# Thresholds on ScalarE, w1 powers in their own place, and one program order for all engines in batch 2

## The chip, the cores and the metric

The kernel runs on one core of a Trainium2 chip. The metric is the device time of one execution in microseconds (us), the median of several executions. The kernel before takes 1797.5 us (four runs, 1794.0 to 1798.6). A ratio below is the mean time of one kernel's fast runs over that of the other's fast runs of the same rounds, so it is not quite the ratio of the medians that are quoted.

The engines are TensorE (PE in the profile; PEld is its weight load), VectorE (DVE), ScalarE (ACT), GpSimd (POOL) and SyncE (SP), which here only issues DMAs.

## The reference

Threshold attention over 8 batches, 8 heads, 576 rows and head size 64, then a Fourier mixing block with a channel MLP. Cut to what matters:

```python
def _attn_ref(q, k, v, tau):
    scores = np.matmul(q, k.transpose(0, 1, 3, 2)) / np.sqrt(q.shape[-1])
    thresh = np.max(scores, axis=-1, keepdims=True) - tau
    scores = np.where(scores >= thresh, scores, -1e9)
    attn = np.exp(scores - np.max(scores, axis=-1, keepdims=True))
    attn = attn / (np.sum(attn, axis=-1, keepdims=True) + 1e-09)
    return np.matmul(attn, v)

def _moe_ref(x, w_ch1, w_ch2):           # x: (8, 576, 512)
    u = x + np.real(fft(fft(x, axis=1), axis=2))
    un = (u - mean(u)) / np.sqrt(var(u) + 1e-06)
    return u + np.maximum(un @ w_ch1, 0.0) @ w_ch2
```

The two weights come as float64. The chip has to turn them into float32 itself, from their integer halves: mask of the mantissa, copy, low bits, exponent, power of two, sign, two multiplies. That is the "conversion" below. w1 has 16 chunks of 128x512 and w2 has 16.

## The kernel before

A batch is 20 "slots": 4 head pairs of 5 row steps, the fifth of 64 rows. Batch 1 (slots 0 to 19) is written in program order by hand and converts w1. In batch 2 (slots 20 to 39) the channel work of the first rows (matmuls `ph` on `u_t` and w1) runs between the attention slots, and w2 is converted. Here the kernel before holds only TensorE to program order; a scheduler orders the other engines.

```python
    def w2_chunk(j):
        c = 2 * (j % 2)
        raw = u_t[:, c : c + 2, S : S + WC].bitcast(INT32)   # unused columns of u_t
        run = convert(w_ch2[128 * j : 128 * (j + 1), :], w2[j][:, :], raw, nc.gpsimd)
        next(run, None)                                      # issues the load
        return run
    # ... scores(i): transposed scores on TensorE, maxima on VectorE, then
        nc.vector.tensor_scalar(out=thr[:, 0:nh], in0=neg[:, 0:nh], scalar1=-1.0,
                                scalar2=thr_off[:, :], op0=ALU.mult, op1=ALU.add)
        # exp on ScalarE, masked sum on VectorE, +1e-9, reciprocal
    # ... channels(g)
                nc.tensor.matmul(ph[:, 0:GT], w1[c][:, 128 * j : 128 * (j + 1)],
                                 u_t[:, c, c0 : c0 + GT], start=(c == 0), stop=(c == ND - 1))
    # ... batch 2 and later
    chunks = [w2_chunk(j) for j in range(2)]
    by_hand.close()
    ctx.enter_context(tc.manual_schedule(engines={mybir.EngineType.PE}))
    for i in range(per_batch, total + 1):
        if i < total:
            scores(i)
        fill()                                # ph and other channel work
        transposed_weights(i - 1)
        # ...
        if i > per_batch and chunks:
            with tc.issue_after(behind[0].ins):
                for _ in chunks.pop(0):       # a whole chunk
                    pass
            if i - per_batch + 1 < NJ:
                chunks.append(w2_chunk(i - per_batch + 1))
```

A raw chunk lies in two rows of `u_t`, in columns 576 to 1087 of each. `ph` reads columns 0 to 383. No byte is shared, yet a chunk's range from its first to its last byte encloses the columns that `ph` reads in the second row.

## Time and profile before

The stages, cut at the start of the scores of slots 20, 24, 37 and 40 (us, from the profile):

| stage | length | TensorE busy | granted clock |
|---|---|---|---|
| batch 1, slots 0 to 19 | 142.3 | 121.1 | 0.95 |
| slots 20 to 23 (mixing of batch 1) | 48.7 | 34.2 | 0.86 |
| slots 24 to 36 (ph and w2 conversion) | 124.4 | 101.1 | 0.88 |
| slots 37 to 39 | 17.6 | 16.8 | 1.00 |
| from slot 40 | 1463.0 | 1454.8 | 1.00 |

From slot 40 on TensorE is 99% busy. Three of these rows as the profile has them (columns: length; busy us and count of TensorE, weight loads, VectorE, ScalarE, GpSimd; granted clock, DMA share, GB/s):

```profile
0.00:142.34 142.34, 121.09 (x600) 68.44 (x600) 113.80 (x251) 83.53 (x148) 86.75 (x148) 0.95 0.36 100
...
191.06:315.50 124.44, 101.09 (x492) 60.68 (x491) 75.32 (x169) 63.77 (x122) 61.09 (x80) 0.88 0.21 65
...
333.12:1796.00 1462.88, 1454.80 (x6496) 833.53 (x6495) 587.81 (x1465) 446.63 (x936) 192.88 (x408) 1.00 0.08 21
```

### The profile page before, as it was taken

How to read it: one execution, taken by the hardware profiler on the slowest of the kernel's cores; microseconds unless marked ns; L12 is line 12 of the kernel's file. 1: busy time of each engine (PE TensorE's matmuls, PEld its weight loads, DVE VectorE, ACT ScalarE, POOL GpSimd, SP SyncE). 2: the span in 40 equal slices, each digit the busy share in tenths (PEclk: the TensorE clock that was granted, in tenths of full speed). 3: DMA queues.
4: the chain of work that ended last, by engine and by line, in shares of the span. 5: the costliest groups of instructions: out<-in, count | busy, mean ns of one | idle time of the engine just before them, and what ended most of it. 6: DMA issues, size and time to landing. Idle time of an engine off the chain costs nothing.

```text
span 1796.1 us, 21623 instructions
## 1 busy us (share of the span) xinstructions
PE 1728.0 (96%) x7872; PEld 995.9 (55%) x7872; DVE 820.5 (46%) x1985; ACT 626.5 (35%) x1270; POOL 368.1 (20%) x669
## 2 busy tenths in 40 slices
PE   8987787999999999999999999999999999999999
PEld 4545454556556656556556556555556565655453
DVE  7987574634334545544324545543434455521010
ACT  5654464334223334333224333432323333411010
POOL 5664564121110111112101031103011031110000
PEclk9989898999999999999999999999999999999999
DMA  5322122100010110100001110110001010000000
GB/s 153 106 57 68 55 73 67 33 26 20 7 38 14 26 33 14 34 26 20 13 26 27 26 27 20 27 32 14 14 26 27 19 27 20 1 12 6 12 6 18
DMA packets 130352, 57.03 MB, mean 32 GB/s; under 512 B 121123, under 2 KB 121125, under 8 KB 130246
## 3 DMA queue, kind: packets, MB, share of 16 engines
q1 hardware_dynamic: 126550, 46.96, 10.0%
q0 software_dynamic: 2304, 8.39, 1.4%
q8 instruction: 63, 1.03, 0.2%
q10 hardware_dynamic: 1392, 0.30, 0.1%
q14 instruction: 43, 0.35, 0.1%
HBM read 46.02 MB, written 9.44 MB: 31 GB/s over the span
## 4 chain that ended last, share of the span: by engine, by line
PE 86%; DVE 8%; ACT 3%; issue 1%; DMA 1%; SPq 1%; POOL 1%; ACTq 0%; DVEq 0%; POOLq 0%
PE ph L685 27%; PE po L706 27%; PE pv L503 9%; PE sc L394 7%; PE pw L482 6%; PE sc L405 2%; DVE e L429 2%; DVE neg L416 1%; PE py L594 1%; PE pa L611 1%; PE pe L468 1%; PE pn L669 1%; ACT e L426 1%; PE pa L615 1%; PE pe L469 1%
## 5 line engine op out<-in xcount | busy, mean ns | idle before, releaser
L685 PE MATMUL ph<-u_t,w 128*128 128x384 f32 x1536 | 531.8, 496 | 27.9 <-ACT u_t L303 27.1
L706 PE MATMUL po<-w,h 128*128 128x512 f32 x1152 | 524.2, 597 | 0.0
L685 PEld LDWEIGHTS ph<-u_t,w 128*128 128x128 f32 x1536 | 285.1, 192 | 220.0 <-ACT u_t L303 26.9
L426 ACT ACTIVATE e<-sc,neg 128x576 f32<-128x576 f32 x288 | 204.2, 738 | 487.0 <-DVE neg L416 485.6
L416 DVE TENSOR_REDUCE neg<-sc 128x1 f32<-128x576 f32 x288 | 205.8, 751 | 317.3 <-PE sc L394 226.8
L706 PEld LDWEIGHTS po<-w,h 128*128 128x128 f32 x1152 | 208.0, 190 | 222.0 <-issue 220.9
L429 DVE SCALAR_TENSOR_TENSOR e<-sc,thr,e 128x576 f32<-128x576 f32 x288 | 225.9, 815 | 39.2 <-ACT e L426 26.0
L438 POOL COPY rec<-den 128x128 f32<-128x128 f32 x160 | 50.2, 314 | 769.5 <-DVE den L436 443.1
L394 PE MATMUL sc<-kT,qT 64*128 64x288 f32 x1024 | 169.6, 442 | 5.3 <-DVE e L429 4.0
L482 PE MATMUL pw<-ident,e 128*128 128x128 f32 x1152 | 157.0, 276 | 10.8 <-DVE x L508 3.4
L691 ACT ACTIVATE h<-ph 128x384 f32<-128x384 f32 x96 | 47.0, 490 | 290.6 <-PE ph L685 290.6
L484 ACT COPY e_t<-pw 128x512 f32<-128x512 f32 x256 | 139.0, 592 | 7.4 <-PE pw L482 3.6
L394 PEld LDWEIGHTS sc<-kT,qT 64*128 64x128 f32 x1024 | 93.6, 192 | 85.4 <-issue 61.1
L482 PEld LDWEIGHTS pw<-ident,e 128*128 128x128 f32 x1152 | 132.7, 142 | 14.5 <-ACT tmp L626 4.1
L693 DVE TENSOR_SCALAR h<-ph 128x384 f32<-128x384 f32 x96 | 53.3, 555 | 184.1 <-PE ph L685 183.8
L508 DVE TENSOR_TENSOR x<-pv,ends 128x288 f32<-128x288 f32 x64 | 29.0, 455 | 172.4 <-PE pv L503 172.4
L472 ACT COPY ends<-pe 128x256 f32<-128x256 f32 x128 | 47.7, 373 | 138.0 <-PE pe L469 129.4
L713 DVE SCALAR_TENSOR_TENSOR u<-po,rstd,u 128x512 f32<-128x512 f32 x36 | 26.9, 748 | 132.4 <-PE po L706 132.4
L503 PE MATMUL pv<-e_t,v_in 128*64 128x288 f32 x512 | 68.3, 409 | 0.0
L503 PE MATMUL pv<-e_t,v_rev 128*64 128x288 f32 x512 | 68.3, 409 | 0.0
L420 DVE TENSOR_SCALAR thr<-neg,thr_off 128x2 f32<-128x2 f32 (+1 forms) x160 | 52.0, 325 | 5.2
L442 POOL COPY e<-e 128x64 f32<-128x64 f32 x32 | 7.8, 242 | 226.6 <-DVE e L429 163.3
(143 smaller groups left out, 1543.5 us busy)
## 6 DMA issues: line engine op xcount, KB each, us to landing
out_dram<-u SPq DMA_DIRECT2D x36, 256.0 KB, 2.0
qk_in<-in_q_dram SPq DMA_DIRECT2D x64, 128.0 KB, 2.4
stage<-in_moe_w_ch_dram SPq DMA_DIRECT2D x16, 512.0 KB, 4.2
v_in<-in_v_dram SPq DMA_DIRECT2D x64, 128.0 KB, 2.3
u_t<-in_moe_w_ch_dram POOLq DMA_DIRECT2D x16, 512.0 KB, 3.9
qk_in<-in_k_dram SPq DMA_DIRECT2D x31, 128.0 KB, 2.4
qk_in<-in_k_dram SPq DMA_DIRECT2D x31, 64.0 KB, 2.3
qk_in<-in_k_dram SPq DMA_DIRECT2D x93, 16.0 KB, 2.0
```

What stands on the lines that cost most here:

```text
L394: nc.tensor.matmul(sc[j][:, c, 0:HALF], qT[hp, 128 * t : 128 * t + 128], kT[hp, HALF * c : HALF * (c + 1)], start=True, stop=True,)
L416: nc.vector.tensor_reduce(out=neg[:, j : j + 1], in_=sc[j][:, :, 0:HALF], axis=AXIS_XY, op=ALU.max, negate=True,)
L420: nc.vector.tensor_scalar(out=thr[:, 0:nh], in0=neg[:, 0:nh], scalar1=-1.0, scalar2=thr_off[:, :], op0=ALU.mult, op1=ALU.add,)
L426: nc.scalar.activation(out=ej, in_=sc[j][:, :, 0:HALF], func=ACT.Exp, bias=neg[:, j : j + 1], scale=1.0)
L429: nc.vector.scalar_tensor_tensor(out=ej, in0=sc[j][:, :, 0:HALF], scalar=thr[:, j : j + 1], in1=ej, op0=ALU.is_ge, op1=ALU.mult, accum_out ...
L438: nc.gpsimd.tensor_copy(rec[:, :].rearrange("p (j d) -> p j d", j=nh), _repeated(den[:, 0:nh], 2 * D // nh))
L482: nc.tensor.transpose(pw[:, c, :], e[:, c0 : c0 + 128], ident[:, :])
L484: nc.scalar.copy(e_t[:, 4 * j : 4 * j + 4, qs], pw[:, :, :])
L503: nc.tensor.matmul(pv[64 * j : 64 * j + 64, 0:HALF], vt[:, 2 * c + j, :], e_t[:, 4 * j + c, cols] if c < 4 else ends[:, 0, cols], start=(c ...
L685: nc.tensor.matmul(ph[:, 0:GT], w1[c][:, 128 * j : 128 * (j + 1)], u_t[:, c, c0 : c0 + GT], start=(c == 0), stop=(c == ND - 1),)
L693: nc.vector.tensor_relu(ht, ph[:, 0:GT])
L706: nc.tensor.matmul(po[:, :], hT[j // 4][:, j % 4, 128 * t : 128 * (t + 1)], w2[j][:, :], start=(j == 0), stop=(j == NJ - 1),)
```

## The change

It means to free VectorE in batch 1 (threshold on ScalarE, exponents taken early, folding and centring spread over several steps) and to keep the hand-made order of all engines through batch 2. The w2 loads move from GpSimd's queue to SyncE's. The cuts leave out three smaller parts: in batch 1 the weighted values of a head pair now stand between the two halves of a slot's softmax, a slot that is filled up with dummy matmuls has one instead of two from slot 16 on, and the mixing of batch 1 is begun a step earlier. The core of the diff, with cuts:

```diff
-        nc.vector.tensor_scalar(
-            out=thr[:, 0:nh], in0=neg[:, 0:nh], scalar1=-1.0, scalar2=thr_off[:, :],
-            op0=ALU.mult, op1=ALU.add,
-        )
         for j in range(nh):
             # exp of half j on ScalarE
+            if j == 0:
+                nc.scalar.activation(
+                    out=thr[:, 0:nh], in_=neg[:, 0:nh], func=ACT.Identity,
+                    bias=thr_off[:, :], scale=-1.0,
+                )
             # masked sum of half j on VectorE, and now +1e-9 for each half
@@ convert (w1 gets its own place for the powers; w2 stays in place)
-        queue.dma_start(out=raw, ...)
+        nc.sync.dma_start(out=raw, ...)
         # mask of the mantissa
+        if not in_place:
+            exponents()
@@ the 64-row slot
-            nc.gpsimd.tensor_copy(e[:, S : S + 64], e[:, 512:S])
+            nc.scalar.copy(e[:, S : S + 64], e[:, 512:S])
@@ batch 2
-    by_hand.close()
-    ctx.enter_context(tc.manual_schedule(engines={mybir.EngineType.PE}))
     for i in range(per_batch, total + 1):
+        if i == 2 * per_batch:
+            by_hand.close()
+            ctx.enter_context(tc.manual_schedule(engines={mybir.EngineType.PE}))
         if i < total:
             scores(i)
+        under_way = [chunks[m] for m in (i - per_batch, i - per_batch - 1) if m in chunks]
+        for run in under_way:          # mask of chunk j; low bits, exponents of chunk j - 1
+            next(run, None)
         fill()
         transposed_weights(i - 1)
+        for run in under_way:          # copy of chunk j; power and sign of chunk j - 1
+            next(run, None)
         # ...
+        j = i - per_batch - 1
+        if j in chunks:
+            next(chunks.pop(j), None)  # the two multiplies of chunk j on GpSimd
+            if j + 2 < NJ:
+                chunks[j + 2] = w2_chunk(j + 2)
```

More of the change, by code (lines that the diff above doesn't have):

```diff
@@ L268, with convert @@
     nc.vector.memset(shift[:], -float((1023 - 127) << 23))
-    def convert(src, dst, raw, queue):
+    def convert(src, dst, raw, power):
         if src.dtype == FP32:
-            queue.dma_start(out=dst, in_=src)
+            nc.sync.dma_start(out=dst, in_=src)
             return
-        queue.dma_start(out=raw, in_=src.bitcast(INT32).rearrange("p (c n) -> p c n", c=2))
+        nc.sync.dma_start(out=raw, in_=src.bitcast(INT32).rearrange("p (c n) -> p c n", c=2))
         pairs = raw.rearrange("p c (n two) -> p c n two", two=2)
@@ L280, in convert, with add_low, exponents, powers_and_signs @@
         bits = dst.bitcast(INT32)
+        in_place = power is None
+        power = low if in_place else power.rearrange("p (c n) -> p c n", c=2)
+        sign = high.bitcast(FP32)
+        def add_low():
+            nc.vector.scalar_tensor_tensor(
+                out=dst, in0=low.bitcast(UINT32), scalar=2.0**-52, in1=dst,
+                op0=ALU.mult, op1=ALU.add,
+            )
+        def exponents():
+            nc.vector.tensor_scalar(
+                out=power, in0=high, scalar1=20, scalar2=0x7FF,
+                op0=ALU.logical_shift_right, op1=ALU.bitwise_and,
+            )
+        def powers_and_signs():
+            nc.scalar.activation(
+                out=power, in_=power, func=ACT.Relu, bias=shift[:, :], scale=float(1 << 23)
+            )
+            nc.scalar.activation(out=sign, in_=high, func=ACT.Sign)
         yield
@@ L285, in convert @@
         )
+        if not in_place:
+            exponents()
         yield
         nc.scalar.activation(out=dst, in_=bits, func=ACT.Copy, bias=1.0, scale=2.0**-20)
+        if not in_place:
+            powers_and_signs()
         yield
-        nc.vector.scalar_tensor_tensor(
-            out=dst, in0=low.bitcast(UINT32), scalar=2.0**-52, in1=dst, op0=ALU.mult, op1=ALU.add
-        )
-        nc.vector.tensor_scalar(
-            out=low, in0=high, scalar1=20, scalar2=0x7FF,
-            op0=ALU.logical_shift_right, op1=ALU.bitwise_and,
-        )
-        yield
-        nc.scalar.activation(
-            out=low, in_=low, func=ACT.Relu, bias=shift[:, :], scale=float(1 << 23)
-        )
-        sign = high.bitcast(FP32)
-        nc.scalar.activation(out=sign, in_=high, func=ACT.Sign)
+        add_low()
+        if in_place:
+            exponents()
+        yield
+        if in_place:
+            powers_and_signs()
         yield
-        nc.gpsimd.tensor_tensor(out=dst, in0=dst, in1=low.bitcast(FP32), op=ALU.mult)
+        nc.gpsimd.tensor_tensor(out=dst, in0=dst, in1=power.bitcast(FP32), op=ALU.mult)
         nc.gpsimd.tensor_tensor(out=dst, in0=dst, in1=sign, op=ALU.mult)
@@ L310, in w1_chunk @@
         cols = slice(WC * g, WC * (g + 1))
-        stage = sb.tile([128, 2, WC], INT32, tag=f"h{n % 4}", bufs=1, name="stage")
-        run = convert(w_ch1[128 * c : 128 * (c + 1), cols], w1[c][:, cols], stage, nc.sync)
+        stage = sb.tile([128, 3, WC], INT32, tag=f"h{n % 4}", bufs=1, name="stage")
+        run = convert(
+            w_ch1[128 * c : 128 * (c + 1), cols], w1[c][:, cols], stage[:, 0:2, :], stage[:, 2, :]
+        )
         next(run, None)
@@ L319, in w2_chunk @@
         raw = u_t[:, c : c + 2, S : S + WC].bitcast(INT32)
-        run = convert(w_ch2[128 * j : 128 * (j + 1), :], w2[j][:, :], raw, nc.gpsimd)
+        run = convert(w_ch2[128 * j : 128 * (j + 1), :], w2[j][:, :], raw, None)
         next(run, None)
@@ L326 @@
     means = {}
+    prs = {}
     def column_means(g):
@@ L338, in mirrored @@
         cols = slice(WC * g, WC * (g + 1))
-        means[g] = means[g], []
+        prs[g] = []
         for c in (1, 3):
@@ L342, in mirrored @@
             nc.tensor.matmul(pr[:, :], mirror[:, :], w1[c][:, cols], start=True, stop=True)
-            means[g][1].append(pr)
+            prs[g].append(pr)
     def less_mean(eng, g, c):
         cols = slice(WC * g, WC * (g + 1))
-        mean, prs = means[g]
-        rows = prs[c // 2][:, :] if c % 2 else w1[c][:, cols]
-        eng.tensor_tensor(out=w1[c][:, cols], in0=rows, in1=mean[:, :], op=ALU.subtract)
+        rows = prs[g][c // 2][:, :] if c % 2 else w1[c][:, cols]
+        eng.tensor_tensor(out=w1[c][:, cols], in0=rows, in1=means[g][:, :], op=ALU.subtract)
     heads = {}
     steps = {}
-    behind = [None]
     xs = {}
@@ L382, in prep_pair, with scores @@
             load_pair(n + 1)
-    def scores(i):
+    def scores(i, between=None):
         n, t = divmod(i, NT)
@@ L419, in scores @@
             )
-        nc.vector.tensor_scalar(
-            out=thr[:, 0:nh], in0=neg[:, 0:nh], scalar1=-1.0, scalar2=thr_off[:, :],
-            op0=ALU.mult, op1=ALU.add,
-        )
         for j in range(nh):
@@ L428, in scores @@
             )
+            if j == 0:
+                nc.scalar.activation(
+                    out=thr[:, 0:nh], in_=neg[:, 0:nh], func=ACT.Identity,
+                    bias=thr_off[:, :], scale=-1.0,
+                )
             nc.vector.scalar_tensor_tensor(
@@ L432, in scores @@
             )
-        nc.vector.tensor_scalar(
-            out=den[:, 0:nh], in0=den[:, 0:nh], scalar1=1e-9, scalar2=None, op0=ALU.add
-        )
-        behind[0] = nc.vector.reciprocal(den[:, 0:nh], den[:, 0:nh])
+            nc.vector.tensor_scalar(
+                out=den[:, j : j + 1], in0=den[:, j : j + 1], scalar1=1e-9, scalar2=None,
+                op0=ALU.add,
+            )
+            if between is not None:
+                between()
+                between = None
+        nc.vector.reciprocal(den[:, 0:nh], den[:, 0:nh])
         rec = sb.tile([128, 2 * D], FP32, tag="rec", name="rec")
@@ L531, in fold_rows @@
             eng.tensor_tensor(out=half[:, c, 1:HALF], in0=up, in1=down, op=op)
+        yield
         for c, c0, op in (
@@ L547, in fold_rows @@
         )
+        yield
         if n % NPAIR == 1:
@@ L755, in step @@
         n, t = divmod(i, NT)
-        scores(i)
         if t == 1 and n > 0:
-            weighted_values(n - 1)
+            scores(i, lambda: weighted_values(n - 1))
             load_v(n + 1)
+        else:
+            scores(i)
+        if t == 1 and n > 0:
+            pass
         elif later and later[0][0] <= i:
-            later.pop(0)[1]()
+            later.pop(0)[1](i)
         else:
-            busy(2)
+            busy(2 if i < NCHUNK else 1)
         if t == NT - 1:
@@ L773, in step @@
                 next(chunks[k], None)
-        while after:
-            after.pop(0)()
+        while after and after[0][0] <= i:
+            after.pop(0)[1]()
         if i - 1 in chunks:
@@ L779, in step @@
             chunks[i + 3] = w1_chunk(i + 3)
-        if t == 3 and n > 0:
-            fold_rows(n - 1)
+        if t == 2 and n > 0:
+            folds.append(fold_rows(n - 1))
+        if folds and next(folds[0], True):
+            folds.pop(0)
+    folds = []
     later = []
@@ L787, in center, with first, second @@
     def center(g):
-        def first():
+        def first(i):
             column_means(g)
-            after.append(lambda: copy_mean(g))
-        def second():
+            after.append((i, lambda: copy_mean(g)))
+        def second(i):
             mirrored(g)
-            for c in range(ND):
-                after.append(lambda c=c: less_mean(nc.vector if c % 2 else nc.gpsimd, g, c))
+            for c, eng, wait in (
+                (1, nc.vector, 0), (3, nc.vector, 0), (0, nc.gpsimd, 1), (2, nc.gpsimd, 2)
+            ):
+                after.append((i + wait, lambda c=c, eng=eng: less_mean(eng, g, c)))
         later.append((ND * g + 6, first))
@@ L820 @@
     while later:
-        later.pop(0)[1]()
+        later.pop(0)[1](per_batch)
     while after:
-        after.pop(0)()
-    chunks = [w2_chunk(j) for j in range(2)]
-    by_hand.close()
-    ctx.enter_context(tc.manual_schedule(engines={mybir.EngineType.PE}))
+        after.pop(0)[1]()
+    while folds:
+        if next(folds[0], True):
+            folds.pop(0)
+    chunks = {j: w2_chunk(j) for j in range(2)}
     for i in range(per_batch, total + 1):
+        if i == 2 * per_batch:
+            by_hand.close()
+            ctx.enter_context(tc.manual_schedule(engines={mybir.EngineType.PE}))
         if i < total:
             scores(i)
+        under_way = [chunks[m] for m in (i - per_batch, i - per_batch - 1) if m in chunks]
+        for run in under_way:
+            next(run, None)
         fill()
@@ L837 @@
         fill()
-        if i > per_batch and chunks:
-            with tc.issue_after(behind[0].ins):
-                for _ in chunks.pop(0):
-                    pass
-            j = i - per_batch + 1
-            if j < NJ:
-                chunks.append(w2_chunk(j))
+        j = i - per_batch - 1
[3 more added lines that the diff above has]
+                chunks[j + 2] = w2_chunk(j + 2)
         fill()
@@ L847 @@
             weighted_values(n - 1)
-            fold_rows(n - 1)
+            for _ in fold_rows(n - 1):
+                pass
             if n + 1 < B * NPAIR:
@@ L853 @@
             mixes.append(mixing(b))
+            if b == 0:
+                next(mixes[0])
             todo += MIX
```

## The prediction

> **What bounds the kernel now.** I read the page's slices first, then busy time in hand-chosen stretches, then the waits of TensorE, then the instructions in order of time.
>
> ```profile
> PE   8987787999999999999999999999999999999999
> PEclk9989898999999999999999999999999999999999
> ```
>
> TensorE has room only in the first seven slices of 44.9 us. Cut by stage (columns: busy us of TensorE, weight loads, VectorE, ScalarE, GpSimd, then granted clock, DMA share, GB/s):
>
> ```profile
> 45.00:142.00 97.00, 84.48 (x446) 48.44 (x446) 81.95 (x175) 59.30 (x106) 62.40 (x79) 0.93 0.27 75
> 142.00:191.00 49.00, 34.51 (x206) 23.35 (x205) 31.11 (x73) 22.21 (x45) 24.10 (x29) 0.86 0.27 74
> 191.00:316.00 125.00, 101.65 (x495) 61.13 (x496) 75.79 (x171) 63.77 (x122) 61.24 (x81) 0.88 0.21 65
> ...
> 331.00:1796.00 1465.00, 1456.92 (x6504) 834.41 (x6502) 588.80 (x1467) 448.34 (x940) 192.88 (x408) 1.00 0.08 21
> ```
>
> A "slot" is one 128-row step of attention, 20 to a batch. Batch 1 (slots 0 to 19) ends near 142 us: VectorE is busy 84% and does scores and w1 conversion in one queue. Slots 24 to 36 of batch 2 lie between 191 and 316 us: TensorE idles 23.4 us and runs at clock 0.88. After 331 us it is 99% busy. So the end is "end of batch 2 plus a fixed 1465 us", and only the first 331 us can change.
>
> What TensorE waits for from 155 to 331 us (total, times, longest):
>
> ```profile
> PE ph L685 <- ACT u_t L303: 27.1, 9, 5.5
> PE py L594 <- DVE den L433: 4.9, 1, 4.9
> ```
>
> L303 is the last ScalarE step of converting a w2 chunk, which lies raw in unused columns of u_t. The channel matmuls (ph) read other columns of u_t, yet wait for it. One such wait in order of time (start, us):
>
> ```profile
> 272.77 2.29 PE L394 MATMUL sc<-kT,qT 64*128 64x288 f32 x8
> 275.09 1.42 DVE L416 TENSOR_REDUCE neg<-sc 128x1 f32<-128x576 f32 x2 [4.55 <-PE sc L394]
> ...
> 280.05 0.16 DVE L436 RECIPROCAL den<-den 128x2 f32<-128x2 f32 x1
> 280.12 0.41 DVE L283 TENSOR_SCALAR w<-u_t 128x512 int32<-128x512 int32 x1
> ...
> 281.23 0.69 DVE L289 SCALAR_TENSOR_TENSOR w<-u_t,w 128x512 f32<-128x512 uint32 x1 [0.70 <-ACT w L287]
> 282.02 0.43 DVE L294 TENSOR_SCALAR u_t<-u_t 128x512 int32<-128x512 int32 x1
> 282.48 0.74 ACT L299 ACTIVATE u_t<-u_t,shift 128x512 int32<-128x512 int32 x1 [1.29 <-DVE u_t L294]
> 283.13 0.65 ACT L303 ACTIVATE u_t<-u_t 128x512 f32<-128x512 int32 x1
> ...
> 283.83 4.21 PE L685 MATMUL ph<-u_t,w 128*128 128x384 f32 x6 [3.62 <-ACT u_t L303]
> ```
>
> Scores, softmax on VectorE, conversion, then ph, one after the other in one slot; and ph then takes 4.21 us for what took 2.10 at 265.97 us. The wait also costs clock.
>
> In batch 1 the threshold op shows a second cost:
>
> ```profile
> L294 DVE TENSOR_SCALAR stage<-stage 128x512 int32<-128x512 int32 x15 | 9.7, 645 | 0.5
> L420 DVE TENSOR_SCALAR thr<-neg,thr_off 128x2 f32<-128x2 f32 x14 | 9.5, 682 | 0.5
> ...
> L420 DVE TENSOR_SCALAR thr<-neg,thr_off 128x1 f32<-128x1 f32 x4 | 0.9, 214 | 0.1
> ```
>
> Two elements take 682 ns on average, one takes 214: beside 1.29 us GpSimd multiplies the two-element op stands waiting.
>
> **What the Trainium skill says.** "SBUF — State Buffer", Who interferes with whom: two-port VectorE ops such as tensor_scalar and GpSimd take a shared port pair in turn, each for a whole instruction. The 682 against 214 ns agrees. "TensorE: Matmul & The Clock Gate", Part 1: after an idle window of about 3.4 us the array falls to half clock until it has been busy as long. Agrees: 3.62 us idle, then 4.21 for 2.10. "ScalarE: Activation LUTs", What ACT_TABLE_LOAD costs: an ACTIVATE with a pointer bias takes about 280 ns plus 0.83 ns an element. No such two-element op is in this trace; I take 0.28 us as an estimate.
>
> **The change, part by part.** I read dependencies from the order and semaphore targets of the built programs, durations from the trace.
>
> *Batch 1.* thr leaves VectorE: 14 x 0.68 us. In its place VectorE waits for ScalarE's exp and then thr: the maxima end 1.42 us after the scores, thr at about 1.75, so about 0.38 us of idling. Gain 14 x 0.3 = 4 us. The +1e-9 becomes two one-element ops (about 0.16 each) for one of 0.24: loss 14 x 0.1 = 1.4. GpSimd starts its multiplies earlier, so mask and exponent ops (586 and 645 ns on average, 0.41 and 0.43 undisturbed) lose perhaps half of their waits: gain 15 x 0.2 = 3. Weighted values now stand between the two halves of a slot: x waits for 5 us of pv matmuls before the second half's mask and all conversion; loss about 0.8 in each of 3 slots, 2.4. Folds and centring in pieces and fewer dummy matmuls are beside VectorE's chain: 0. Sum: 3 us gained.
>
> *Slots 20 to 23.* From VectorE's first sum (170.87) to the ph that can run (187.1) it takes 16.2 us through GpSimd. After: ten adds of 0.75, two multiplies of 1.29, one copy of 0.33, two more adds: about 12. No DMA issue (0.75 each) is left on GpSimd. Gain about 4.
>
> *Slots 24 to 36*, where the result is decided. In the new program order a slot is: scores(i), mask of chunk j, then low bits and exponents of chunk j-1 on VectorE; ScalarE's power and sign of chunk j-1 follow in the same slot. The false dependency stays: all 14 ph groups in slots 24 to 36 wait for a conversion step of their own slot (9 for the sign, and 5, in slots 28 to 32, for the exponent op), and scores(i+1) stand behind ph. Before, the scheduler put most conversions ahead of the next slot's scores; only four groups (slots 24, 32, 33, 34) waited within their slot, and slots like 26, 27 and 36 took about 5.5 us.
>
> The new chain from the end of sc: maxima to reciprocal 1.42 + 0.38 + 2 x 0.82 + small ops 0.65 = 4.1; mask 0.41, low bits 0.70, exponents 0.43: 5.65; power and sign 0.74 + 0.65: 7.1. (The conversion alone: 3.0 instead of 3.65, as the ScalarE round trip inside is gone.) At full clock a slot with one ph matmul left is sc 1.24 + 7.1 + 0.9 = 9.3; with three left, 10.5; a slot that waits for the exponents needs 1.24 + 5.7 + 0.9 to 2.1 + transposes 1.2 = 9.1 to 10.2; a 64-row slot about 1.8 less; pv adds 5.0 to three slots. Summed over the 13 slots, with 1.4 for one preparation, 2.6 for two table loads, and ScalarE late by 1 to 3 us in slots 30 and 32: about 147 us, against 124.4 now (191.13 to 315.50). That is 22 us lost at full clock. Three-matmul slots idle 4 to 5 us, so half clock may add up to 3 us in each of five: up to 15 more.
>
> *After 331 us*: thr and the 64-column copy on ScalarE (35% busy), w2 loads gone from GpSimd's queue: 0.
>
> Sum: -3 - 4 + 22 to 37 = +15 to +30. The walk has no slack in it where a step is out of order, but it contradicts what the author of such a change must hope for, so I lean towards the low end and below it: 1797.6 + 14, about 1812.
>
> **Rivals.** (1) The new order removes the 27.1 us of ph waits: conversion steps are spread and shorter, and all engines follow one order. For it: these waits are the largest idle item. Against: the semaphore targets show the waits still there, and more of them within the slot. It would make 1765 to 1785. (2) Nothing moves: TensorE work is fixed, both orders hide as much; batch 1 gains what batch 2 loses: 1790 to 1802. (3) The full half-clock loss: ph and scores at half speed through all of batch 2: 1830 to 1840.
>
> **Range and chances.** 1812, 8 in 10 between 1780 and 1834. 2% is 36 us: faster by that needs all of rival 1 and more (0.05); slower needs rival 3 (0.12); the rest 0.83.
>
> **What would show it.** In the new profile TensorE's wait of ph for ScalarE's sign op and for VectorE's exponent op should total 35 us or more over 11 or more waits; the stretch of slots 24 to 36 should be 140 us or longer with a granted clock below 0.88; batch 1 should end 0 to 6 us earlier; the stretch after batch 2 should stay 1465 us within 5. I am wrong if that stretch of batch 2 is shorter than 124 us, which would mean the conversion runs ahead of the scores after all, or if batch 1 alone gains over 10 us.

## The result

The changed kernel takes 1845.5 us (median of four runs, 1844.6 to 1848.6), against 1797.5 us. The ratio is 1.0273, with a 95% interval from 1.0255 to 1.0292: slower, and above the range of the prediction.

The page's slices of the profile after. The third to seventh slices are the ones to look at:

```profile
PE   8986656799999999999999999999999999999999
...
PEclk9997778899999999999999999999999999999999
```

One slice is 46.1 us now. TensorE's busy share falls to 5 and 6 tenths and its clock to 7 tenths where the kernel before had 7 to 8 and 8 to 9; everything behind is as before.

The same stretches of the changed kernel, same columns:

```profile
0.00:135.12 135.12, 116.90 (x605) 67.70 (x605) 102.27 (x250) 87.10 (x174) 85.66 (x143) 1.00 0.38 104
...
184.76:360.98 176.22, 116.56 (x491) 66.02 (x490) 70.39 (x169) 67.46 (x140) 52.92 (x68) 0.80 0.17 50
...
377.02:1842.80 1465.78, 1455.04 (x6496) 833.28 (x6495) 557.09 (x1438) 474.94 (x1084) 186.63 (x383) 1.00 0.08 21
```

Batch 1 ends 7.2 us earlier. Slots 24 to 36 hold the same matmuls (491, and 492 before) but take 51.8 us longer: 36.3 us more of idle TensorE (59.7 against 23.4) and 15.5 us more of busy time at the lower clock. From slot 40 on it is 2.8 us longer.

TensorE's longest waits in the first 400 us of the changed kernel (total us, times, longest):

```profile
PE ph L714 <- ACT u_t L304: 31.1, 10, 6.0
PE ph L714 <- DVE u_t L293: 29.2, 5, 9.0
```

L304 is the sign op and L293 the exponent op of a w2 chunk. The kernel before had 27.1 us in 9 waits, all for the sign op. These are 60.3 us in 15 waits. The new order made the wait that it should have removed more frequent.

The longest of them in order of time (start, us, engine; SPq is SyncE's DMA queue):

```profile
249.77 1.28 POOL L326 TENSOR_TENSOR w<-w,u_t 128x512 f32<-128x512 f32 x1
...
251.47 0.16 DVE L463 RECIPROCAL den<-den 128x1 f32<-128x1 f32 x1
...
253.56 0.56 SPq L277 DMA_DIRECT2D u_t<-in_moe_w_ch_dram  x1
257.21 0.43 DVE L308 TENSOR_SCALAR w<-u_t 128x512 int32<-128x512 int32 x1 [5.58 <-DMA u_t<-in_moe_w_ch_dram]
257.55 0.68 DVE L287 SCALAR_TENSOR_TENSOR w<-u_t,w 128x512 f32<-128x512 uint32 x1
258.34 0.43 DVE L293 TENSOR_SCALAR u_t<-u_t 128x512 int32<-128x512 int32 x1
...
258.82 4.21 PE L714 MATMUL ph<-u_t,w 128*128 128x384 f32 x6 [8.97 <-DVE u_t L293]
```

The softmax of the slot is done at 251.6. The mask op (L308) of the next chunk then waits 5.58 us for its raw data, which came only 3.65 us after their load was issued. The last multiply (L326) had freed the buffer at 251.05, and the load was issued at 253.56: q and k loads stood ahead of it on SyncE's queue for these 2.5 us. That part is an exception; the other w2 loads of this stretch were issued at most 0.6 us after their buffer came free. In VectorE's program order the low bits (L287) and the exponents (L293) of the chunk before stand behind that mask, and `ph` stands behind them. In slots 24 to 36 the mask waits for a load four times:

```profile
DVE w L308 <- DMA u_t<-in_moe_w_ch_dram: 10.7, 4, 5.6
```

The kernel before has no such wait in this stretch. This is a second loss beside the one foreseen.

### The profile page after: what moved, and what is told of

Its sections match the earlier page's. It is cut to its first block, busy times and chain, and to the rows that moved or that the text cites. A ratio compares the mean times of both kernels' runs of the same rounds, so it can differ in the third digit from the quotient of the medians.

```text
span 1842.8 us, 21678 instructions
## 1 busy us (share of the span) xinstructions
PE 1739.3 (94%) x7870; PEld 1000.5 (54%) x7870; DVE 768.6 (42%) x1953; ACT 659.6 (36%) x1462; POOL 346.9 (19%) x621
## 4 chain that ended last, share of the span: by engine, by line
PE 80%; DVE 5%; ACT 3%; DMA 1%; POOL 1%; issue 1%; SPq 0%; DVEq 0%; ACTq 0%
PE ph L714 27%; PE po L735 26%; PE pv L530 8%; PE sc L415 6%; PE pw L509 5%; PE sc L426 2%; DMA u_t<-in_moe_w_ch_dram 1%; DVE e L451 1%; PE py L623 1%; DVE neg L437 1%; PE pa L640 1%; ACT e L443 1%; PE pn L698 1%; PE pa L644 1%; PE pe L495 1%; PE pe L496 1%
## 5 line engine op out<-in xcount | busy, mean ns | idle before, releaser
L714 PE MATMUL ph<-u_t,w 128*128 128x384 f32 x1536 | 544.5, 504 | 61.6 <-ACT u_t L304 31.1
L443 ACT ACTIVATE e<-sc,neg 128x576 f32<-128x576 f32 x288 | 211.4, 734 | 540.9 <-DVE neg L437 539.7
L499 ACT COPY ends<-pe 128x256 f32<-128x256 f32 x128 | 47.5, 371 | 95.5 <-PE pe L496 89.0
L558 POOL TENSOR_TENSOR half<-x 128x287 f32<-128x287 f32 x48 | 38.1, 816 | 89.6 <-DVE x L535 62.2
L530 PEld LDWEIGHTS pv<-e_t,v_rev 128*64 128x64 f32 x512 | 36.3, 141 | 33.5 <-issue 10.2
```

The lines of the kernel that those rows point to most:

```text
L443: nc.scalar.activation(out=ej, in_=sc[j][:, :, 0:HALF], func=ACT.Exp, bias=neg[:, j : j + 1], scale=1.0)
L499: nc.scalar.copy(ends[:, :, qs], pe[:, 0:2, :])
L530: nc.tensor.matmul(pv[64 * j : 64 * j + 64, 0:HALF], vt[:, 2 * c + j, :], e_t[:, 4 * j + c, cols] if c < 4 else ends[:, 0, cols], start=(c ...
```

## The experiments

Fourteen kernels ran, each with runs of the kernel before on the same chip. "a_" names start from the changed kernel, "b_" names from the kernel before. All times by stage come from one profile each. Kernels with the changed batch 1 left as it is ended it between 134.4 and 137.8 us, so a single figure of batch 1 is good to about 2 us; the other stages repeat within about 1 us in the few pairs with the same code there (slots 20 to 23 of the changed kernel and a_busy, slots 24 to 36 of the kernel before and b_power).

| kernel | batch 1 | slots 20-23 | 24-36 | 37-39 | from 40 | median us |
|---|---|---|---|---|---|---|
| before | 142.3 | 48.7 | 124.4 | 17.6 | 1463.0 | 1797.5 |
| changed | 135.1 | 49.6 | 176.2 | 16.0 | 1465.8 | 1845.5 |
| a_sched2 | 135.3 | 47.6 | 128.2 | 17.3 | 1466.2 | 1796.8 |
| a_pool_dma | 137.7 | 49.2 | 171.6 | 17.4 | 1465.9 | 1844.5 |
| a_own_raw | 137.8 | 46.2 | 134.0 | 17.3 | 1465.8 | 1799.4 |
| b_own_raw | 143.9 | 47.5 | 106.1 | 17.5 | 1463.1 | 1782.7 |
| a_own3 | 136.6 | 46.3 | 119.1 | 16.0 | 1465.8 | 1785.7 |
| a_thr_dve | 136.7 | 50.1 | 176.2 | 17.4 | 1462.9 | 1845.0 |
| b_thr_act | 137.5 | 47.7 | 128.5 | 17.4 | 1466.1 | 1801.2 |
| b_power | 139.7 | 49.1 | 124.6 | 17.7 | 1463.0 | 1794.5 |
| best | 135.9 | 47.5 | 101.9 | 17.4 | 1463.0 | 1766.7 |
| a_first | 137.0 | 50.3 | 124.2 | 18.5 | 1465.8 | 1795.2 |
| a_busy | 135.8 | 50.6 | 171.1 | 16.0 | 1465.8 | 1841.6 |
| a_own3_thr | 136.3 | 46.3 | 120.4 | 17.2 | 1463.0 | 1783.3 |
| a_noload | 135.6 | 46.8 | 160.2 | 17.5 | 1465.7 | 1831.4 |
| a_noload_busy | 134.4 | 47.7 | 156.5 | 16.0 | 1465.7 | 1823.8 |

**Is it the order of batch 2? (a_sched2)** Batch 2 as in the kernel before, everything else as changed.

```diff
+    chunks = [w2_chunk(j) for j in range(2)]
+    by_hand.close()
+    ctx.enter_context(tc.manual_schedule(engines={mybir.EngineType.PE}))
     for i in range(per_batch, total + 1):
-        if i == 2 * per_batch: ...            # and the under_way steps
+        # a whole chunk behind the reciprocal; loads on nc.gpsimd
```

> The changed kernel with batch 2 as in the kernel before: program order held on TensorE alone from slot 20 on, each w2 chunk converted whole behind the reciprocal, w2 loads on GpSimd's queue. Theory (the loss of 51.8 us in slots 24 to 36 comes from the fixed order of batch 2, and batch 1 keeps its gain of 7.2 us): slots 24 to 36 back to 120 to 130 us, batch 1 still ending near 135 us, 1786 to 1798 us in all. Rival (the loss comes from thresholds on ScalarE or the other single changes, which remain here): slots 24 to 36 stay above 150 us, 1825 us or more.

Measured: 1796.8 us, ratio 1.0000 (0.9985 to 1.0015). Slots 24 to 36 are back to 128.2 us. The loss is in the order of batch 2, with the loads' queue. But the batch 1 gain of 7 us does not show in the total: 3.8 us more in slots 24 to 36 and 3.3 us more after slot 40 eat it. What does that comes below (b_thr_act).

**Is it the loads' queue? (a_pool_dma)** Having seen ten q and k loads ahead of the w2 load on SyncE's queue, I moved it.

```diff
-        nc.sync.dma_start(out=raw, ...)
+        queue = nc.gpsimd if power is None else nc.sync
+        queue.dma_start(out=raw, ...)
```

> The changed kernel with only the w2 loads moved back to GpSimd's queue. Theory (a w2 load on SyncE's queue stands behind ten q and k loads that wait for the pair's transposes, so the raw chunk lands late): VectorE's 10.7 us of waits of the mask op for that load in slots 24 to 36 vanish, and with them some half-clock time: 1825 to 1838 us. Rival (the raw buffer comes free late anyway, so that the queue doesn't matter, and an issue of 0.74 us on GpSimd delays the multiplies): 1843 to 1850 us.

Measured: 1844.5 us. My theory falls and the rival holds: VectorE's waits for loads did not vanish (15.1 us in 7 waits from 130 to 365 us, and 16.7 in 7 in the changed kernel). Its slots 24 to 36 are 4.6 us shorter, but its batch 1 and slots 37 to 39, where nothing was changed, are 4.0 us longer, so a gain is not shown. The Trainium skill, "Trainium Kernel Development and Optimization", Key Constraints, says that DMAs issued from several engines share the same DMA engines and that issuing from more of them saves only issue time. That agrees: a w2 load took 3.8 us from issue to landing on GpSimd's queue and 3.7 on SyncE's, and the times are 1844.5 and 1845.5 us.

**Is it the false dependency? (a_own_raw, b_own_raw)** There is no room for two more buffers of 4 KB per partition. But the last rows of w2 are empty until the last chunks are converted, so raw chunks 0 to 11 can lie there. Chunks 12 to 15 stay in `u_t`. (A first version for 13 chunks gave NaN values.)

```diff
-    w2 = [const.tile([128, DM], FP32, name=f"w2_{j}") for j in range(NJ)]
+    w2_all = const.tile([128, NJ, DM], FP32, name="w2_all")
+    w2 = [w2_all[:, j, :] for j in range(NJ)]
@@ w2_chunk
+        if j < NJ - 4:
+            r = NJ - 4 + 2 * (j % 2)
+            raw = w2_all[:, r : r + 2, :].bitcast(INT32)
```

> The changed kernel with the raw w2 chunks 0 to 11 in the rows of w2 that are filled last, not in unused columns of u_t (chunks 12 to 15 stay in u_t). Theory (the ph matmuls wait for conversions only because both lie in one box of u_t): the waits of ph in slots 24 to 32, 44.8 us in all, fall below 8 us; those of slots 33 to 36, 12.5 us, stay; clock of the stretch rises from 0.80 above 0.9; 1795 to 1815 us. Rival (the fixed order of the engines is what binds: without this wait TensorE waits as long for the softmax of the next slot): less than 15 us gained, 1830 us or more.

> The kernel before with the same move of the raw w2 chunks 0 to 11 out of u_t. Theory (the same false dependency costs the kernel before 14.2 us of waits in slots 25 to 32 and half-clock time behind them): 1775 to 1786 us. Rival (the scheduler's order fills the gap with other work, or the wait is taken over by the softmax): 1790 to 1799 us.

Measured: a_own_raw 1799.4 us, ratio 1.0009 to the kernel before, that is 46 us less than the changed kernel; b_own_raw 1782.7 us, ratio 0.9919 (0.9900 to 0.9937). Both theories hold, but for the clock of the stretch, which came to 0.88 in a_own_raw and not above 0.9. The waits of TensorE in slots 24 to 36 of a_own_raw:

```profile
PE pe L500 <- POOL rec L469: 13.9, 2, 8.0
PE ph L718 <- ACT u_t L305: 13.7, 4, 5.4
```

Only the four chunks left in `u_t` still hold `ph` back. In place of the others a new wait stands first, of the transposes for the broadcast reciprocal. A cause that fits is in VectorE's waits (a_own3 below tests it):

```profile
DVE w_all L309 <- DMA w_all<-in_moe_w_ch_dram: 19.5, 8, 4.7
```

Without the false dependency the slots are shorter, the loads are later relative to them, and VectorE holds the next softmax behind a mask that waits for its data. The same stretch of b_own_raw, columns as in the stage lines above:

```profile
191.30:297.37 106.07, 92.15 (x492) 56.25 (x491) 76.53 (x171) 63.61 (x122) 58.02 (x77) 0.93 0.23 67
```

**Are two raw buffers too few? (a_own3)** One row more for `w2_all`, which the 2 KB left allow, makes three buffers.

```diff
-    w2_all = const.tile([128, NJ, DM], FP32, name="w2_all")
+    w2_all = const.tile([128, NJ + 1, DM], FP32, name="w2_all")
-            r = NJ - 4 + 2 * (j % 2)
+            r = NJ - 5 + 2 * (j % 3)
-    chunks = {j: w2_chunk(j) for j in range(2)}
+    chunks = {j: w2_chunk(j) for j in range(3)}    # and loads issued three chunks ahead
```

> As a_own_raw, with three raw buffers for chunks 0 to 11 in place of two, each load issued three chunks ahead. Theory (a chunk's conversion now spans two slots, so two buffers leave a load only the time from the last multiply to the next slot's mask op, and VectorE stands waiting for the load in order, with the next reciprocal behind it): VectorE's waits of the mask op for loads, 24.9 us in a_own_raw, fall below 6, those of the transposes for the broadcast reciprocal (13.9 us) below 2, slots 24 to 36 from 134 to 112 to 122 us; 1778 to 1790 us. Rival (the waits pass to the softmax of the next scores): no more than 5 us gained, 1794 us or more.

Measured: 1785.7 us, 13.7 us less. Over the first 400 us VectorE's waits for w2 loads fell from 24.9 to 3.2 us, and slots 24 to 36 take 119.1 us. The wait for the reciprocal fell only to 6.5 us, not below 2, so late loads were a part of it and not all:

```profile
DVE w_all L309 <- DMA w_all<-in_moe_w_ch_dram: 3.2, 1, 3.2
...
PE pe L500 <- POOL rec L469: 6.5, 2, 3.7
```

The Trainium skill, "Trainium Kernel Development and Optimization", Best Practices, says to double-buffer. Here a conversion reaches over two slots, and two buffers leave no slot for the load; this run shows that the third is worth 13.7 us.

**What is the threshold worth? (a_thr_dve, b_thr_act)** The threshold op put back, and the threshold op moved alone.

```diff
 # a_thr_dve: threshold on nc.vector ahead of the exponentials, as before
 # b_thr_act: on nc.scalar behind the first exponential, as changed
```

> The changed kernel with the threshold op back on VectorE ahead of the exponentials; everything else stays. Theory (the threshold op gave batch 1 about 4 us): batch 1 ends 3 to 6 us later, at 138 to 142 us; in batch 2 the chain of a slot gets about 0.2 us shorter; 1843 to 1849 us. Rival (thresholds on ScalarE bring nothing in batch 1, and the gain comes from the order of the rest): batch 1 ends at 134 to 137 us and the total falls below 1843 us.

> The kernel before with thresholds on ScalarE behind the first exponential, and nothing else. Theory: batch 1 ends 3 to 5 us earlier than at 142.3; about 2 us are lost after slot 40, where ScalarE gets later; 1792 to 1797 us. Rival (VectorE waits for ScalarE's exponential and threshold as long as its own op took): batch 1 ends at 141 to 144 us, 1798 to 1802 us.

Measured: b_thr_act 1801.2 us, ratio 1.0023 (1.0011 to 1.0035). Batch 1 ends 4.9 us earlier, as expected, but slots 24 to 36 take 4.0 us longer and the part from slot 40 3.1 us longer, so the move alone loses. a_thr_dve 1845.0 us: taking it out of the changed kernel leaves batch 1 at 136.7, which is inside the spread of 134.4 to 137.8, against the theory, and gives the 2.9 us after slot 40 back. So both readings held in part: alone the move gives 4.9 us, beside the rest hardly anything. The group lines of VectorE in the first 135 us fit this, first the kernel before, then the changed kernel (busy us, mean ns, then idle time before and its cause):

```profile
L420 DVE TENSOR_SCALAR thr<-neg,thr_off 128x2 f32<-128x2 f32 x16 | 11.3, 708 | 0.6
...
L451 DVE SCALAR_TENSOR_TENSOR e<-sc,thr,e 128x576 f32<-128x576 f32 x36 | 29.3, 813 | 13.4 <-ACT thr L447 12.9 <-POOL half L558 0.4
...
L308 DVE TENSOR_SCALAR w<-stage 128x512 int32<-128x512 int32 x16 | 7.6, 476 | 1.1 <-DMA stage<-in_moe_w_ch_dram 1.1
```

then a_thr_dve:

```profile
L441 DVE TENSOR_SCALAR thr<-neg,thr_off 128x2 f32<-128x2 f32 x16 | 7.4, 463 | 0.6
```

With the rest of the change in place the threshold op costs VectorE 463 ns and not 708 ns as in the same stretch before, 7.4 us in all. What takes its place is 12.9 us of waiting for ScalarE, where a_thr_dve has 3.6.

**What are the powers worth? (b_power)** Only the w1 powers in their own place.

```diff
-        stage = sb.tile([128, 2, WC], INT32, tag=f"h{n % 4}", bufs=1, name="stage")
+        stage = sb.tile([128, 3, WC], INT32, tag=f"h{n % 4}", bufs=1, name="stage")
 # and convert() of the changed kernel; w2 in place and on nc.gpsimd as before
```

> The kernel before with only the w1 powers in a place of their own, so that VectorE takes the exponents with the mask, a step earlier, and ScalarE does power and sign with the copy. Theory of the prediction (earlier multiplies on GpSimd give about half the waits of mask and exponent ops): batch 1 ends 2 to 3 us earlier, 139 to 140.5 us; 1794 to 1797 us. Rival (this step alone is worth as much as the whole gain of batch 1, as the chain of a chunk loses a round trip): batch 1 ends at 135 to 138 us, 1790 to 1794 us.

Measured: 1794.5 us, ratio 0.9980 (0.9966 to 0.9995), batch 1 at 139.7. Of the parts that were run alone it is the only one that gains in the total. Its 2.7 us in batch 1 are hardly more than the 2 us to which such a figure is good, and the upper end of its interval is close to 1.

**Fixed order, or place in the slot? (a_first)** All engines stay in program order and the raw data stay in `u_t`; the whole conversion of a chunk stands ahead of the slot's scores.

```diff
+        j = i - per_batch - 1
+        if j in chunks:
+            for _ in chunks.pop(j):
+                pass
+            if j + 2 < NJ:
+                chunks[j + 2] = w2_chunk(j + 2)
         if i < total:
             scores(i)
-        under_way = ...                       # and the steps behind
```

> The changed kernel with program order on all engines in batch 2 kept, raw chunks still in u_t, but each chunk converted whole, in one slot, ahead of that slot's scores and softmax. Theory (what costs is the place of the conversion behind the softmax of its own slot, not the fixed order as such): the waits of ph for conversion steps in slots 24 to 36 fall from 57.3 to under 25 us, VectorE's waits for loads vanish since the load gets a slot more, slots 24 to 36 take 125 to 145 us, 1795 to 1815 us. Rival (a fixed order with chunks in u_t costs as much in either place, as the softmax is now late): 1830 us or more.

Measured: 1795.2 us, ratio 0.9985 (0.9970 to 1.0000), slots 24 to 36 in 124.2 us. It came out slightly below the low end of the slots' range. The waits of `ph` for conversion fell from 57.3 to 18.1 us, and VectorE waited for no load:

```profile
PE ph L714 <- ACT u_t L304: 18.1, 9, 4.2
```

A fixed order is not what costs; conversion behind the softmax of its own slot, spread over two slots, is. The run changes the place, the spread and the loads' time at once, so it does not say how much each of them costs; nor was this order tried with the raw data out of `u_t`.

**What does the half clock cost? (a_busy)** Five dummy matmuls a slot keep TensorE busy in its waits.

```diff
             scores(i)
+            if per_batch + 3 < i < 2 * per_batch - 3:
+                busy(5)
```

> The changed kernel with five dummy matmuls behind the scores in slots 24 to 36, so that TensorE does not idle long enough to fall to half clock; all waits stay. Theory (15.5 us of the loss are matmuls at half clock, 116.6 us of busy time for the same 491 matmuls that took 101.1): the granted clock of the stretch rises from 0.80 above 0.9 and the time falls by 5 to 15 us, to 1830 to 1841 us. Rival (the clock does not set the end, as the ends of the slots hang on VectorE's chain alone, or the dummies delay as much as they save): 1843 us or more.

Measured: 1841.6 us, 4 us less, between what theory and rival expected. Its slots 24 to 36, same columns as above:

```profile
186.32:357.43 171.11, 151.80 (x622) 81.63 (x621) 70.19 (x169) 68.30 (x140) 52.55 (x69) 0.95 0.18 51
```

The dummies of the 13 slots take 4.56 us each, 59.3 us, so the real matmuls took about 92.5 us and not 116.6: 24 us of slow matmul time are gone, but the stretch is only 5.1 us shorter. Part of the rest turned into waiting: VectorE's waits for loads rose from 10.7 to 14.6 us. Part is the dummies' own cost. What was left of the waits of `ph`:

```profile
PE ph L714 <- DVE u_t L293: 10.9, 4, 4.7
PE ph L714 <- ACT u_t L304: 8.3, 7, 2.6
```

Three of the 14 groups no longer waited, and in slot 24 the transposes started 5.5 us after the slot's start, directly behind the dummies, where the changed kernel had them after 1.1 us. Slot by slot, six of the 13 slots are longer than in the changed kernel, by 6.3 us in all, and seven are shorter, by 11.5 us. So 5.1 us is a net figure; how much of the half clock was in the shadow of the chain through VectorE is not settled.

**How much is loads, how much the walk? (a_noload, a_noload_busy)** With 12 kernels run, the size was still open. Here the loads of chunks 2 to 15 are left out. The result is wrong; orders and dependencies stay.

```diff
-        nc.sync.dma_start(out=raw, ...)
+        if load:                              # j < 2 for w2
+            nc.sync.dma_start(out=raw, ...)
```

> The changed kernel with the loads of the w2 chunks 2 to 15 left out, so that every conversion works on what an earlier one left in the raw columns; the result is wrong on purpose, order, instructions and false dependency stay. Theory (my walk of slots 24 to 36 took every chunk as landed, and the late loads are the larger part of what it missed): the waits for loads are gone, slots 24 to 36 fall from 176.2 to 150 to 162 us, which is the range of the walk, and the total to 1818 to 1833 us. Rival (loads only fill gaps that the chain has anyway): slots 24 to 36 stay above 168 us, 1838 us or more.

> As a_noload, wrong on purpose too, with the five dummy matmuls of a_busy behind the scores. This is the walk's own case, full clock and every chunk landed, for which it had 147 us. Theory (but for loads and clock the walk was right): slots 24 to 36 take 142 to 152 us; the total is 1805 to 1822 us. Rival (the walk's chain of a slot is itself too short): above 158 us.

Measured: a_noload 1831.4 us, slots 24 to 36 in 160.2 us, as the theory had it: loads cost 16.0 us of the 51.8, with what they cost in clock (TensorE is busy 107.7 us and not 116.6). The waits of `ph` stayed, at 50.2 us against 57.3:

```profile
PE ph L715 <- ACT u_t L305: 30.0, 10, 5.4
PE ph L715 <- DVE u_t L294: 20.2, 5, 5.4
```

a_noload_busy took 1823.8 us in all and 156.5 us for slots 24 to 36, between what theory and rival expected (152 and 158). My walk had 147 us for this very case, so its chain was at most 9.5 us short. Where is not settled. Part may again be the dummies: five slots (24, 26, 30, 34 and 36) are longer than in a_noload, by 5.5 us in all.

**The parts that gain, together (best)** Batch 1 as changed; from slot 20 on the kernel before, with 14 raw chunks in the rows of `w2_all`. a_own3_thr is the same idea in the fixed order: a_own3 with the threshold on VectorE from slot 20.

```diff
 # best = a_sched2 with w2_all of NJ + 1 rows, and
+        by_dve = i >= per_batch               # threshold, 1e-9 and 64-column copy as before
+        if j not in (NJ - 3, NJ - 1):
+            r = NJ - 1 - 2 * (j % 2)
+            raw = w2_all[:, r : r + 2, :].bitcast(INT32)
```

> What the runs so far point to: batch 1 of the changed kernel (thresholds on ScalarE, powers in a place of their own), from slot 20 on the kernel before (program order on TensorE alone, thresholds, sums and the 64-column copy as before), and 14 of the 16 raw w2 chunks in the last rows of w2 instead of u_t. If the parts add up: batch 1 ends at 135 to 138 us (gain 5 to 7), slots 24 to 36 take 98 to 106 us (124.4 before, 106.1 in b_own_raw with 12 chunks moved), after slot 40 1463 us: 1762 to 1774 us. Rival (the parts hide one another): 1778 us or more.

> As a_own3, with the threshold op on VectorE from slot 20 on. Theory (thresholds on ScalarE cost about 4 us in slots 24 to 36 and 3.1 us after slot 40, as b_thr_act shows): the stretch after slot 40 goes back from 1466 to 1463 us; 1777 to 1784 us. Rival (in the fixed order ScalarE is not late, only the 3 us after slot 40 or nothing come back): 1782 to 1787 us.

Measured: best 1766.7 us, ratio 0.9827 (0.9812 to 0.9842), and correct: 31 us below the kernel before and 79 below the changed one. The parts add up, as expected. Its slots 24 to 36:

```profile
183.41:285.33 101.92, 90.29 (x491) 55.40 (x490) 76.64 (x171) 63.45 (x122) 59.12 (x79) 0.97 0.26 75
```

Of 101.9 us TensorE is busy 90.3, at clock 0.97. a_own3_thr 1783.3 us: the 2.8 us after slot 40 came back, and slots 24 to 36 got 1.3 us longer instead of shorter, which is the rival's case.

## Why the prediction was right or wrong

The sum of the prediction and what the profiles show (us, negative is a gain):

| term | predicted | measured |
|---|---|---|
| batch 1 | -3 | -7.2 |
| slots 20 to 23 | -4 | +0.9 |
| slots 24 to 36 | +22 to +37 | +51.8 |
| slots 37 to 39 | 0 | -1.6 |
| from slot 40 | 0 | +2.8 |
| sum | +15 to +30 | +46.7 |

**The mechanism was right.** The false dependency stays, nearly every `ph` group waits for a conversion step of its own slot, for the sign or the exponent op, and the stretch with the conversion decides. All 14 groups of slots 24 to 36 waited as the prediction said. a_own_raw (46 us back by moving raw data alone) and a_first (50 us back by converting each chunk whole, ahead of the scores, which also gives its load a slot more) show both halves of it: a false dependency, and a conversion placed so that it bites.

**The step that failed is the walk of slots 24 to 36, "Summed over the 13 slots ... about 147 us".** It had no term for the loads: each chunk was taken as landed. The measured term is 16.0 us (a_noload). It follows from the change: a conversion over two slots with two buffers frees a buffer only at the end of the slot before the one that needs it. The semaphore targets that I read show that a mask waits for a load, but not that the load is late. The rest of the walk's chain was at most 9.5 us short, of which up to 5.5 may be the dummies of a_noload_busy; where is open.

**The half-clock term may have been too large.** "Up to 15 more" was the right amount of slow matmul time (15.5 us more busy), but not all of it need be path: removing it gave 5.1 us in a_busy, and 3.7 us where a_noload_busy stands against a_noload. Both are net of what the dummies cost; the slots that got shorter gained 11.5 and 9.2 us. I counted busy time as path without asking what the engine would have waited for. 147 + 9.5 + 3.7 + 16.0 is the measured 176.2, but by construction: these are the differences between the profiles.

**The lean was wrong.** "I lean towards the low end and below it" took the point to +14, just below my own sum, for the reason that it went against the author's hope. The dependencies had been read from the built program, and that hope was no measurement. But the sum itself, 1813 to 1828 us, would have been low as well.

**Batch 1** gained 7 us, not 3 (4.5 to 7.9 us over the spread of the changed kernels): the threshold alone 4.9 us (predicted 4), the powers alone 2.7 us (predicted 3, by earlier multiplies), and all but the threshold already 5.7 us. Whether these parts hide one another is not shown, as figures that are good to 2 us cannot tell. The losses that I set against this, 2.4 us for the weighted values between the halves and 1.4 us for the split sum, were not tested alone.

**Slots 20 to 23.** GpSimd's adds ran as walked: from the first to the last of them 12.1 us (167.84 to 179.97), and 12 were predicted. From VectorE's first sum to the `ph` that can run it took 13.7 us, and 16.2 before. But that sum came 32.2 us after the start of the stretch (at 167.30), where the kernel before had it after 28.5 us. Ahead of it VectorE had waited 2.9 and 1.7 us for w2 loads, and the kernel before has no such wait there. So the missing load term fits here as well, though no run shows it alone; a_noload, in which the second of these waits is gone, has 46.8 us. The wait of `ph` for a sign op did not grow (3.0 us, and 5.5 before).

**From slot 40** "0" was wrong by 2.8 us. b_thr_act and a_thr_dve, which have it and lack it, show that it is the threshold on ScalarE. ScalarE is busy 32% of that time, but the listed waits of TensorE for its copies rose from 3.3 to 6.1 us.

**The checks named in advance:** `ph` waits of 35 us or more in 11 or more waits (60.3 in 15), 140 us or more at a clock below 0.88 (176.2 at 0.80), the end stage 1465 us within 5 (1465.8): met. Batch 1 0 to 6 us earlier: missed by 1.2, which is within the spread of that stage.

## What to carry to other kernels

Before fixing an order by hand, look for waits between tiles that share a buffer but no bytes; moving the data added no instruction here and was worth 15 us before any reordering. When a pipeline is stretched over one more step, count its buffers again, and give each load its time in the walk of a slot. Busy time lost to a low clock need not all be on the path, so ask first what the engine was waiting for; and dummy work that keeps the clock up shows only a net figure, since it can stand in the way itself.

## What the Trainium skill lacked or had wrong

- "Trainium Kernel Development and Optimization", Best Practices, has double-buffering as the rule. It lacks that a chunk processed over two steps needs a third buffer: 24.9 against 3.2 us of waits for loads, and 1799.4 against 1785.7 us.
- "TensorE: Matmul & The Clock Gate", Part 1, has the half clock right (4.21 us for what took 2.10), but lacks how little of it may show in the time: 24 us less of real matmul time, from 116.6 to 92.5 us, shortened the stretch by 5.1 us, net of what the dummy matmuls cost.
- No page has the false dependency of two ranges in one tile that enclose but don't touch each other: 46 us in the changed kernel and 15 us in the kernel before.
- No page has what an added small ScalarE op costs TensorE when it waits for ScalarE's copies: about 3 us over the 120 slots from slot 40 on. The op itself took 292 ns, close to the 0.28 us that the prediction estimated from the skill.
